# The maximum across blocks in a two-part attention and Fourier kernel: two transposes on TensorE in place of five small VectorE copies

## The chip, the cores and the metric

The kernel runs on one core of a Trainium2 chip. The metric is the device time of one execution in microseconds. Three runs of the kernel before took 1163.07 us in the median (1162.79 to 1165.32).

A core has five engines, each with its own queue of instructions that it works through in order: TensorE (PE) multiplies matrices and writes to PSUM, VectorE (DVE) and ScalarE (ACT) work on rows and read or write PSUM and SBUF, GpSimd (POOL) works on SBUF alone, and SyncE (SP) issues the transfers (DMA) here. They wait for each other by semaphores. PSUM has eight banks of 128 partitions x 512 floats. A matrix product holds one operand, the weights, in the array (its load is PEld in the profile) and streams the other.

## The reference, cut to what matters

```python
# part A: Fourier mixing, real part of a DFT over hidden (448) and sequence (2048)
a = einsum("bsd,ed->bse", x, dft_hid_re);  b = einsum("bsd,ed->bse", x, dft_hid_im)
y = einsum("ts,bse->bte", dft_seq_re, a) - einsum("ts,bse->bte", dft_seq_im, b)
# part B: attention, 16 heads of 28
q, k, v = split(x @ wqkv)
p = softmax(einsum("bhqd,bhkd->bhqk", q, k) * 28 ** -0.5)
o = einsum("bhqk,bhkd->bhqd", p, v)  ->  @ wo
out = concatenate([y, attention], axis=-1)       # (1, 2048, 896), float32
```

The inputs of part B are scaled by 8 each, so the scores are large and the softmax needs the maximum of each query's row.

## The kernel before, in words

Products are made in split precision: an operand is divided into a high part and a remainder, and two or three products are summed. Part A (`hidden`, `sequence`, lines 547 and 662) and the projections of part B (`project`, `values`, line 547) run as fill work in two PSUM banks (`fill_s`); the attention uses the other six (`bank_s`).

The attention is cut into units (h, c): a head and a chunk of 512 queries, 64 in all. Twenty units are `unit_twice`: the scores are computed once with queries on partitions for their maxima (line 754, maximum at 758), the maxima are transposed on TensorE (line 717), and the scores are computed again with the maximum subtracted inside the product (line 786). The other 44 are `unit_kept`, where the change lies. There the scores are computed once, keys on partitions and queries along the row: 16 tiles of 128 keys x 512 queries (line 808). ScalarE copies each tile to SBUF (line 813, through the helper at 415), and VectorE keeps a running elementwise maximum `rm` (lines 815 and 818), so `rm[p, n]` is the maximum over all keys whose number is p modulo 128.

What remains is a maximum over the 128 partitions for each query, and its spread to all partitions. Before, VectorE does all of it, in two PSUM banks `o` and `pm`. Number the queries n = 32 j + c (j below 16, c below 32) and the partitions p = 32 i + r (i below 4, r below 32).

1. Line 823 transposes `rm` in blocks of 32 x 32: `o[32 i + c, 32 j + r]` is the maximum of query 32 j + c at partition 32 i + r.
2. Line 825 takes the maximum over r and negates it: `pm[32 i + c, j]`, 128 x 16. What is left is a minimum over the four blocks i of partitions.
3. Line 830, three copies: blocks 1, 2 and 3 of 32 partitions are put beside block 0. Line 835 takes the minimum over the four: 32 x 16.
4. Line 833, two copies: the result is copied from 32 partitions to 64 and from 64 to 128.
5. Line 841 transposes in blocks once more, each column repeated 32 times, so that every partition of `pm` holds the negated maximum of all 512 queries.

ScalarE copies `pm` to `mb` in SBUF (line 843). GpSimd adds `mb` to the kept scores (line 858), or VectorE adds `pm` for some pairs of tiles; ScalarE takes the exponential (line 862); TensorE multiplies by the values (line 735, `pv_group`), in the narrow form of 32 columns of weights. `unit_out` copies the result out and `out_of` (877) folds and scales it.

The order of all instructions is written out before the launch by a list scheduler, `Schedule.run`. Each step has a cost on its engine, a latency after which others see it (`lat`), and a due time (`key`); of the steps that are ready on an engine, the one due first is taken. `RAW` is the time that the scheduler leaves after a VectorE step before a VectorE step that depends on it (`own=RAW`). `LANES`, `FLOW` and the `extra` of a transfer say when the scheduler thinks that a transfer lands. `Piece` (lines 515 to 537) loads a block of weights: a transfer to `wraw`, ScalarE's copy to `whi` (line 516), GpSimd's remainder `wlo` (line 522). In `project`, ScalarE copies a finished bank's high part (line 588) and VectorE writes the remainder (line 589), which frees the bank.

Of the kernel before, what the change touches and what calls it, by code (L numbers as in the profile page):

```python
# [11 lines left out]
F32 = mybir.dt.float32  # L12
F32R = mybir.dt.float32r
AF = mybir.ActivationFunctionType
ALU = mybir.AluOpType
AX = mybir.AxisListType
# [8 lines left out]
P = 128  # L25
NT = S // P
# [21 lines left out]
def f32(ap):  # L48
    return ap.bitcast(F32)
# [4 lines left out]

RAW = 0.16
LANES = 8
FLOW, FLOW_IN = 200.0, 400.0
T_IN = 20.0  # L60
# [257 lines left out]
def tile_kernel(ctx, tc, xa, wre, wim, wd, xb, wqkv, wo, out):  # L318
    nc = tc.nc
# [5 lines left out]
    sch = Schedule()  # L325

    def new(name, shape, dtype=F32, n=None, in_turn=False):
        if n is None:
            return sb.tile(shape, dtype, tag=name, name=name)
        sch.pools.append(Slots([sb.tile(shape, dtype, tag=f"{name}{i}", name=f"{name}{i}") for i in range(n)], in_turn))  # L330
        return sch.pools[-1]
# [10 lines left out]
    ident = new("ident", [P, P])  # L342
# [14 lines left out]
    sm_s = new("sm", [P, NT], F32, 1)  # L357
    mx_s = new("mx", [P, 4, NC], F32, 1)
    nm_s = new("nm", [P, 4], F32, 3)
    n2_s = new("n2", [64, P], F32R, 1)  # L360
    banks = [ps.tile([P, CH], F32, tag=f"bank{i}", name=f"bank{i}") for i in range(8)]

    w_first = Weights(lent, held=True)
# [23 lines left out]


    M512, M448, MS = 0.2335, 0.2065, 0.2365
    ACT_P, ACT_S, DVE_P, POOL_2, SMALL = 0.48, 0.52, 0.60, 1.25, 0.11  # L390

    def pe(key, emit, n=1, d=MS, lat=0.25, **kw):
        return sch.add({"PE": n * d}, key, emit, lat=lat, **kw)

    def dma(key, emit, size=256, extra=0.0, n=1, **kw):

        return sch.add({"SP": 0.4}, key, lambda e: emit(), dmas=[(size, extra)] * n, **kw)
# [4 lines left out]
    def dve(key, emit, d=DVE_P, **kw):  # L402
        return sch.add({"DVE": d}, key, lambda e: emit(), **kw)
# [105 lines left out]
    class Piece:  # L509


        def __init__(self, src, key, kind="c", early=False):
            self.hi, self.lo = whi.slot(), wlo.slot()
            raw = wraw.slot()
            ld = dma(key, lambda: nc.sync.dma_start(raw.t, src()), acq=[raw])
            a = act(key + (0 if early else 1), lambda: nc.scalar.activation(self.hi.t, raw.t, AF.Copy), ACT_S,  # L516
                    deps=[ld], acq=[self.hi], use=[raw])
            at = key + (0 if early else 1.5)
            both = ("DVE",) if early else ("POOL",)
            e = {g: {"DVE": 0.8, "POOL": 1.25}[g] for g in both}  # L520
            n = 4 if kind == "c" else 3
            b = sch.add(e, at, lambda g: eng[g].tensor_tensor(  # L522
                self.lo.t[:, :n], raw.t[:, :n], f32(self.hi.t)[:, :n], op=ALU.subtract),
                deps=[a], acq=[self.lo], use=[raw, self.hi])
            self.ready, self.hi_ready, self.lo_ready = [b], a, [b]
            if kind == "x":
                self.ready.append(sch.add({g: {"DVE": 0.3, "POOL": 0.53}[g] for g in both}, at, lambda g: eng[g].tensor_tensor(
                    self.hi.t[64:, 3], raw.t[64:, 3], f32(self.hi.t)[64:, 3], op=ALU.subtract),
                    deps=[a], use=[raw, self.hi]))
            elif kind == "w":  # L530
                self.ready.append(sch.add({g: {"DVE": 0.3, "POOL": 0.53}[g] for g in both}, at, lambda g: eng[g].tensor_tensor(
                    self.lo.t[:64, 3], raw.t[:64, 3], f32(self.hi.t)[:64, 3], op=ALU.subtract),
                    deps=[a, b], use=[raw, self.hi, self.lo]))
                self.ready.append(sch.add({"DVE": 0.15, "POOL": 0.25}, at, lambda g: eng[g].memset(
                    f32(self.lo.t)[64:, 3], 0.0), deps=[b], use=[self.lo]))
                self.lo_ready = self.ready
# [258 lines left out]
    def unit_kept(u):  # L795
        h, c = u
        t_a, t_b, dt = due[u]
        q = q_s.slot()
        lq = load_q(u, q)
        rm, mb = rm_s.slot(), mb_s.slot()  # L800
        kept, cs = [], []
        for kt in range(NT):
            o = bank_s.slot()
            if kt % 2 == 0:
                kept.append(kept_s.slot())
            s = Half(kept[-1], kt % 2)
            key = t_a + kt * dt
            m = pe(key, lambda e, o=o, kt=kt: nc.tensor.matmul(  # L808
                o.t, KT[h][kt // 4].t[:KR, kt % 4 * P:(kt % 4 + 1) * P], q.t[:KR, :], start=True, stop=True),
                deps=[*lq, *got_k[h, kt // 4], before.get("ka")], use=[o, s.pair, rm, q, KT[h][kt // 4]])  # L810
            in_line("ka", m)
            cs.append(sch.add({"ACT": ACT_P, "DVE": DVE_P} if kt == 1 else {"ACT": ACT_P}, key - 20,
                              lambda e, o=o, s=s: copy_of(e, s.t, o.t), deps=[m], use=[o, s.pair], lock=[o]))
            if kt == 1:
                prev = dve(key - 20, lambda o=o, s=kept[0]: nc.vector.tensor_tensor(rm.t, o.t, s.t[:, 0, :], op=ALU.max),
                           deps=[m, cs[0]], use=[rm, o, kept[0]], lock=[o], own=RAW)
            elif kt:
                prev = dve(key - 20, lambda o=o: nc.vector.tensor_tensor(rm.t, o.t, rm.t, op=ALU.max),  # L818
                           deps=[m, prev], use=[rm, o], lock=[o], own=RAW)
        key = t_a + 16 * dt - 20  # L820

        o = bank_s.slot()
        t = dve(key, lambda o=o: nc.vector.transpose(o.t, rm.t), 0.64, deps=[prev], acq=[o], use=[rm])  # L823
        pm = bank_s.slot()
        r = dve(key, lambda o=o: nc.vector.tensor_reduce(
            pm.t[:, :NT], o.t.rearrange("p (j r) -> p j r", r=32), axis=AX.X, op=ALU.max, negate=True), deps=[t], use=[o, pm], own=RAW)


        def beside(i):
            return lambda: nc.vector.tensor_copy(pm.t[:32, i * NT:(i + 1) * NT], pm.t[32 * i:32 * i + 32, :NT])  # L830

        def back(n, o=o):
            return lambda: nc.vector.tensor_copy(o.t[n:2 * n, :NT], o.t[:n, :NT])
        r = [dve(key, beside(i), SMALL, deps=[r], use=[pm], own=RAW) for i in (1, 2, 3)]
        r = dve(key, lambda o=o: nc.vector.tensor_reduce(
            o.t[:32, :NT], pm.t[:32, :4 * NT].rearrange("p (i j) -> p j i", i=4), axis=AX.X, op=ALU.min), 0.17,
            deps=r, use=[pm, o], own=RAW)
        for n in (32, 64):
            r = dve(key, back(n), SMALL, deps=[r], use=[o], own=RAW)

        t = dve(key, lambda o=o: nc.vector.transpose(pm.t, o.t[:, :NT].unsqueeze(2).to_broadcast([P, NT, 32])), 0.64,  # L841
                deps=[r], use=[pm, o], own=RAW)
        ld = act(key, lambda: nc.scalar.activation(mb.t, pm.t, AF.Copy), deps=[t], use=[pm, mb], lock=[pm])  # L843
        po = bank_s.slot()
        last_pv = None
        pairs = NT // 2

        def over_pair(t):
            return bass.AP(tensor=t.tensor, offset=t.offset, ap=[t.ap[0], [0, 2], [1, CH]])

        for g in range(NT // GV):
            es = []
            for i in range(GV // 2 * g, GV // 2 * (g + 1)):
                s = kept[i]
                key = t_b + 2 * i * dt

                def shift(e, s=s):
                    eng[e].tensor_tensor(s.t, s.t, over_pair(pm.t if e == "DVE" else mb.t), op=ALU.add)  # L858
                on_dve = i < DVE_SHIFT or due[u][0] > T_END - LATE
                sh = sch.add({"POOL": 2.36, "DVE": 1.13} if on_dve else {"POOL": 2.36}, key, shift,  # L860
                             deps=[ld, t, cs[2 * i], cs[2 * i + 1]], use=[s, mb, *([pm] if on_dve else [])])
                es.append(act(key, lambda s=s: nc.scalar.activation(s.t, s.t, AF.Exp, scale=SCALE), 0.96, deps=[sh], use=[s]))  # L862
            last_pv = pv_group(u, g, kept[GV // 2 * g:GV // 2 * (g + 1)], [*es, last_pv], po, key)
        unit_out(u, po, last_pv, key - 20)
# [33 lines left out]
    o = bank_s.slot()  # L898
# [18 lines left out]
    key = fkey(0, 0)  # L917
# [5 lines left out]
    key = fkey(0, 0)  # L923
# [19 lines left out]
    for n, c in enumerate(LAST):  # L943
        raws = []
        for k in range(4):
            pair = kept_s.slot()
            raw = Half(pair, 0)
            key = T_OUT + n
            deps = [o_done[h, c] for h in range(H) if (h + 1) * DH > k * P and h * DH < (k + 1) * P] + [before["ka"]]
            if k < 3:  # L950
                ld = dma(key, lambda raw=raw, k=k, c=c: nc.sync.dma_start(raw.t, on_d[k * P:(k + 1) * P, c * CH:(c + 1) * CH]),
                         deps=deps, use=[pair])
            else:
# [3 lines left out]
                ld = dma(key, twice, 128, n=2, deps=deps, use=[pair])  # L957
            raws.append((raw, ld))
        for i in range(2):
            x = [kt_s.slot() for _ in range(4)]  # L960
            ready = []
            for k in range(4):
                raw, ld = raws[k]
# [69 lines left out]
```

## Time and profile before

| | |
|---|---|
| median of 3 runs | 1163.07 us |
| the profiled execution | 1163.75 us |
| its span, first to last instruction | 1161.9 us |
| mean granted TensorE clock | 0.999 |
| TensorE busy | 1145.3 us (99%) |
| VectorE busy | 1010.8 us (87%) |
| ScalarE busy | 1029.1 us (89%) |
| GpSimd busy | 884.6 us (76%) |

In the profile an engine's busy time is the time in which it has an instruction in work. TensorE's products overlap, and their ends are modelled, so the distance between the starts of two products is a better measure of what one costs than its own length. A row of a group gives the line, the engine, the operation, the tiles out<-in, shapes and count, then the busy time, the mean length of one in ns, and the time that the engine had been idle before them, with what ended it. A row of the timeline gives the start, the length, and the instruction, and in brackets the idle time before it and what ended it. The second profile below has other line numbers: lines after 360 move by three, those after the reduction by one less.

### The profile page before, as it was taken

The numbers are of one execution on the slowest core, as the hardware profiler recorded it, in microseconds if no ns is written. First come the engines' busy times: TensorE is split into PE (matmuls) and PEld (weight loads), VectorE is DVE, ScalarE is ACT, GpSimd is POOL, SyncE is SP. The second block draws the span as 40 slices with busy tenths as digits, with TensorE's granted clock in tenths as the row PEclk, the third lists the DMA queues.
The fourth block names the chain that finished last, engine by engine and source line by source line (L and its number), as shares of the span: only waits on it lengthen the run. The fifth ranks groups of instructions, "written<-read, shape, count | busy, mean of one in ns | idle before, by whom it ended". The sixth has DMA issues, their size and how long they took to land.

```text
span 1161.9 us, 19485 instructions
## 1 busy us (share of the span) xinstructions
PE 1145.3 (99%) x6110; PEld 778.7 (67%) x6110; DVE 1010.8 (87%) x1803; ACT 1029.1 (89%) x1748; POOL 884.6 (76%) x521
## 2 busy tenths in 40 slices
PE   8999999999999999999999999999999999999998
PEld 7876556656676667767666656566666667766677
DVE  6599989999898989999899999998989998799832
ACT  5269999999999899999899999999999999899952
POOL 2138687888789888978888897987989899596630
PEclk9999999999999999999999999999999999999999
DMA  8893344222223222232333232232423223323543
GB/s 259 176 214 120 125 140 148 66 83 73 82 85 102 85 85 82 73 114 78 89 105 100 86 96 65 85 101 90 120 80 96 88 87 114 120 73 92 162 158 109
DMA packets 111880, 125.19 MB, mean 108 GB/s; under 512 B 49368, under 2 KB 63352, under 8 KB 111776
## 3 DMA queue, kind: packets, MB, share of 16 engines
q1 hardware_dynamic: 111776, 123.94, 35.8%
q8 instruction: 48, 0.79, 0.3%
q14 instruction: 56, 0.46, 0.1%
HBM read 90.00 MB, written 33.77 MB: 107 GB/s over the span
## 4 chain that ended last, share of the span: by engine, by line
PE 79%; DVE 9%; ACT 5%; DMA 3%; issue 3%; SPq 0%; DVEq 0%; ACTq 0%
PE bank L662 25%; PE bank L735 17%; PE bank L808 13%; PE bank L547 8%; PE bank L786 6%; PE bank L754 5%; DVE rm L818 4%; PE bank L987 3%; ACT kept L415 2%; DMA kept<-xb 1%; PE bank L877 1%; DVE mx L758 1%; ACT kept L790 1%; ACT kept L862 1%; DVE bank L823 1%
## 5 line engine op out<-in xcount | busy, mean ns | idle before, releaser
L858 POOL TENSOR_TENSOR kept<-kept,mb 128x1024 f32<-128x1024 f32 x254 | 605.7, 2409 | 93.7 <-ACT mb L843 85.6
L818 DVE TENSOR_TENSOR rm<-bank,rm 128x512 f32<-128x512 f32 x616 | 421.7, 685 | 53.7 <-PE bank L808 17.3
L415 ACT ACTIVATE kept<-bank 128x512 f32<-128x512 f32 (+1 forms) x661 | 381.0, 625 | 59.4 <-PE bank L808 34.4
L862 ACT ACTIVATE kept<-kept 128x1024 f32<-128x1024 f32 x341 | 361.2, 1102 | 7.8 <-DVE kept L858 5.0
L662 PE MATMUL bank<-big,whi 128*128 128x448 f32 x1024 | 325.3, 368 | 0.0
L522 POOL TENSOR_TENSOR wlo<-wraw,whi 128x512 fp32r<-128x512 f32 (+1 forms) x166 | 204.2, 1233 | 131.3 <-ACT whi L516 94.8
L808 PE MATMUL bank<-q,k 84*128 84x512 f32 x704 | 277.2, 414 | 2.6 <-DVE bank L841 1.6
L735 PE MATMUL bank<-kept,v 128*32 128x512 f32 x1944 | 240.7, 597 | 1.3 <-DVE mx L758 0.7
L758 DVE TENSOR_REDUCE mx<-bank 128x1 f32<-128x512 f32 x320 | 216.0, 681 | 8.6 <-PE bank L754 7.2
L662 PEld LDWEIGHTS bank<-big,whi 128*128 128x128 f32 x1024 | 193.3, 189 | 32.4 <-issue 5.9
L662 PE MATMUL bank<-big,wlo 128*128 128x448 f32 x512 | 188.4, 368 | 0.2 <-POOL wlo L522 0.2
L808 PEld LDWEIGHTS bank<-q,k 84*128 84x128 f32 x704 | 130.1, 189 | 86.8 <-issue 19.5
L790 ACT ACTIVATE kept<-bank 128x512 f32<-128x512 f32 x290 | 179.3, 637 | 4.1 <-PE bank L786 3.5
L735 PEld LDWEIGHTS bank<-kept,v 128*32 128x32 f32 x1944 | 56.4, 109 | 123.7 <-issue 110.9
L786 PE MATMUL bank<-q,k 86*128 86x512 f32 x320 | 127.4, 408 | 0.7 <-DMA q<-nmd 0.6
L754 PE MATMUL bank<-k,q 84*128 84x512 f32 x320 | 127.3, 407 | 0.3 <-DVE n L767 0.3
L516 ACT ACTIVATE whi<-wraw 128x512 fp32r<-128x512 f32 x167 | 110.8, 667 | 15.3 <-DMA wraw<-wqkv 12.1
L858 DVE TENSOR_TENSOR kept<-kept,bank 128x1024 f32<-128x1024 f32 x87 | 104.1, 1210 | 5.3 <-ACT mb L843 4.9
L662 PEld LDWEIGHTS bank<-big,wlo 128*128 128x128 f32 x512 | 96.9, 189 | 14.5 <-issue 1.0
L547 PE MATMUL bank<-wd,whi 128*128 128x448 f32 x256 | 79.6, 373 | 1.4 <-ACT kept L415 1.1
L786 PEld LDWEIGHTS bank<-q,k 86*128 86x128 f32 x320 | 59.8, 188 | 31.5 <-DVE rm L818 8.1
L754 PEld LDWEIGHTS bank<-k,q 84*128 84x128 f32 x320 | 60.0, 188 | 26.5 <-issue 4.2
(81 smaller groups left out, 1081.1 us busy)
## 6 DMA issues: line engine op xcount, KB each, us to landing
wraw<-wre SPq DMA_DIRECT2D x64, 256.0 KB
wraw<-wim SPq DMA_DIRECT2D x64, 256.0 KB
qkd<-wd SPq DMA_DIRECT2D x32, 256.0 KB
wraw<-xa SPq DMA_DIRECT2D x32, 256.0 KB
k<-qkd SPq DMA_DIRECT2D x64, 112.0 KB
q<-qkd SPq DMA_DIRECT2D x64, 112.0 KB
qkd<-kept SPq DMA_DIRECT2D x24, 256.0 KB
out<-kept SPq DMA_DIRECT2D x27, 224.0 KB
```

The lines of the kernel that those rows point to most:

```text
L415: nc.scalar.activation(dst, src, AF.Copy)
L522: b = sch.add(e, at, lambda g: eng[g].tensor_tensor(self.lo.t[:, :n], raw.t[:, :n], f32(self.hi.t)[:, :n], op=ALU.subtract), deps=[a], acq ...
L662: nc.tensor.matmul(o.t[:, :D], a.t[:, k, :], b[:, q * 4 + k, :], start=(q == 0 and k == 0 and j == 0), stop=(q == 3 and k == 3 and j == 2))
L735: nc.tensor.matmul(o.t[j * VW:(j + 1) * VW, :], VT[h].t[:, kt // 4, j, :], pairs[i // 2].t[:, i % 2, :], start=(kt < 4), stop=(kt >= NT - 4))
L754: m = pe(key, lambda e, o=o, kc=kc, qt=qt: nc.tensor.matmul(o.t, q.t[:KR, qt * P:(qt + 1) * P], KT[h][kc].t[:KR, :], start=True, stop=True ...
L758: ms.append(dve(key - 20, lambda o=o, kc=kc, qt=qt: nc.vector.tensor_reduce(mx.t[:, qt, kc:kc + 1], o.t, axis=AX.X, op=ALU.max), deps=[m], ...
L786: m = pe(key, lambda e, o=o, kt=kt: nc.tensor.matmul(o.t, KT[h][kt // 4].t[:KR + 2, kt % 4 * P:(kt % 4 + 1) * P], q.t[:KR + 2, :], start=T ...
L790: es.append(act(key - 20, lambda o=o, p=p: nc.scalar.activation(p.t, o.t, AF.Exp, scale=SCALE), deps=[m], use=[o, p.pair]))
L808: m = pe(key, lambda e, o=o, kt=kt: nc.tensor.matmul(o.t, KT[h][kt // 4].t[:KR, kt % 4 * P:(kt % 4 + 1) * P], q.t[:KR, :], start=True, sto ...
L818: prev = dve(key - 20, lambda o=o: nc.vector.tensor_tensor(rm.t, o.t, rm.t, op=ALU.max), deps=[m, prev], use=[rm, o], lock=[o], own=RAW)
L858: eng[e].tensor_tensor(s.t, s.t, over_pair(pm.t if e == "DVE" else mb.t), op=ALU.add)
L862: es.append(act(key, lambda s=s: nc.scalar.activation(s.t, s.t, AF.Exp, scale=SCALE), 0.96, deps=[sh], use=[s]))
```

## The change

Steps 3 and 4 above are replaced. The 128 x 16 maxima of step 2 are written to a small SBUF tile `m`. TensorE transposes it to 16 x 128 (`o[j, 32 i + c]`), so that the four blocks i lie beside each other along the row. One VectorE minimum over i reads them four times over (a broadcast axis) and writes 16 x 128 to the SBUF tile `mr`, already repeated for the four blocks of partitions. TensorE transposes this back to 128 x 16, into columns 128 to 143 of the bank `o`, and step 5 reads it from there. The tile `mr` shares a 128 x 128 tile, `small`, with `n2`, the maxima's tile of `unit_twice`: `n2` has partitions 0 to 63, `mr` has 64 to 79.

Two constants of the scheduler change too: `RAW` goes from 0.16 to 0.20, and the transfers of pieces due between 1 and 80 us are thought to land 6 us later.

```diff
-RAW = 0.16
+RAW = 0.20
...
-    n2_s = new("n2", [64, P], F32R, 1)
+    small = new("small", [P, P], F32R)
+    n2_s, mr_s = Slots([small[:64]]), Slots([f32(small)[64:64 + NT]])
+    sch.pools += [n2_s, mr_s]
+    m_s = new("m", [P, NT], F32, 1)
...
-            ld = dma(key, lambda: nc.sync.dma_start(raw.t, src()), acq=[raw])
+            ld = dma(key, lambda: nc.sync.dma_start(raw.t, src()), extra=6 if 1 < key < 80 else 0.0, acq=[raw])
...
         t = dve(key, lambda o=o: nc.vector.transpose(o.t, rm.t), 0.64, deps=[prev], acq=[o], use=[rm])
+        mq, mr = m_s.slot(), mr_s.slot()
+        r = dve(key, lambda o=o: nc.vector.tensor_reduce(
+            mq.t, o.t.rearrange("p (j r) -> p j r", r=32), axis=AX.X, op=ALU.max, negate=True), 0.61, deps=[t], use=[o, mq])
+
+        t = pe(key, lambda e, o=o: nc.tensor.transpose(o.t[:NT, :P], mq.t, ident), d=0.11, deps=[r], use=[o, mq])
+        r = dve(key, lambda o=o: nc.vector.tensor_reduce(
+            mr.t.rearrange("j (a c) -> j a c", a=4),
+            o.t[:NT, :P].rearrange("j (i c) -> j c i", i=4).unsqueeze(1).to_broadcast([NT, 4, 32, 4]), axis=AX.X, op=ALU.min),
+            0.62, deps=[t], use=[o, mr])
+        t = pe(key, lambda e, o=o: nc.tensor.transpose(
+            o.t[:, P:P + NT], mr.t, ident[64:64 + NT, 64:64 + NT]), d=0.11, deps=[r], use=[o, mr])
+
         pm = bank_s.slot()
-        r = dve(key, lambda o=o: nc.vector.tensor_reduce(
-            pm.t[:, :NT], o.t.rearrange("p (j r) -> p j r", r=32), axis=AX.X, op=ALU.max, negate=True), deps=[t], use=[o, pm], own=RAW)
-        def beside(i):
-            return lambda: nc.vector.tensor_copy(pm.t[:32, i * NT:(i + 1) * NT], pm.t[32 * i:32 * i + 32, :NT])
-        def back(n, o=o):
-            return lambda: nc.vector.tensor_copy(o.t[n:2 * n, :NT], o.t[:n, :NT])
-        r = [dve(key, beside(i), SMALL, deps=[r], use=[pm], own=RAW) for i in (1, 2, 3)]
-        r = dve(key, lambda o=o: nc.vector.tensor_reduce(
-            o.t[:32, :NT], pm.t[:32, :4 * NT].rearrange("p (i j) -> p j i", i=4), axis=AX.X, op=ALU.min), 0.17,
-            deps=r, use=[pm, o], own=RAW)
-        for n in (32, 64):
-            r = dve(key, back(n), SMALL, deps=[r], use=[o], own=RAW)
-        t = dve(key, lambda o=o: nc.vector.transpose(pm.t, o.t[:, :NT].unsqueeze(2).to_broadcast([P, NT, 32])), 0.64,
-                deps=[r], use=[pm, o], own=RAW)
+        t = dve(key, lambda o=o: nc.vector.transpose(pm.t, o.t[:, P:P + NT].unsqueeze(2).to_broadcast([P, NT, 32])), 0.64,
+                deps=[t], use=[pm, o])
```

2 lines of the change are left out of this document (1 added, 1 removed).

## The prediction

> **What bounds the kernel now.** I read the page from its top: shares of the span, the slices, the chain. Then the stretches of time, the waits of TensorE, and the groups that the change touches.
>
> ```profile
> PE 1145.3 (99%) x6110; PEld 778.7 (67%) x6110; DVE 1010.8 (87%) x1803; ACT 1029.1 (89%) x1748; POOL 884.6 (76%) x521
> ...
> PE   8999999999999999999999999999999999999998
> ...
> PE 79%; DVE 9%; ACT 5%; DMA 3%; issue 3%; SPq 0%; DVEq 0%; ACTq 0%
> ```
>
> TensorE is busy for 99% of the span, in every slice but the first and the last, and holds 79% of the chain. A busy TensorE need not be one at its peak, so the stretches and its waits come next (columns: window, length, busy time of PE, PEld, DVE, ACT, POOL with counts, clock, DMA share, GB/s).
>
> ```profile
> 100.00:200.00 100.00, 99.10 (x510) 60.47 (x508) 94.14 (x166) 94.60 (x162) 78.90 (x45) 1.00 0.39 135
> 200.00:300.00 100.00, 96.44 (x499) 62.64 (x496) 93.33 (x164) 95.68 (x167) 85.01 (x58) 0.98 0.24 71
> 300.00:500.00 200.00, 199.40 (x1108) 134.15 (x1110) 181.46 (x322) 190.67 (x320) 169.91 (x90) 1.00 0.29 88
> 900.00:1050.00 150.00, 150.00 (x834) 101.69 (x827) 134.67 (x243) 139.86 (x235) 128.83 (x69) 1.00 0.32 97
> ```
>
> From 300 us on TensorE hardly pauses (0.6 us in 200, none in 150), while VectorE has some 10% to spare. Who does hold TensorE up (waits of PE: for whom, us in total, times, longest)?
>
> ```profile
> PE bank L547 <- DVE kept L589: 2.5, 1, 2.5
> PE bank L808 <- DVE bank L841: 1.6, 2, 0.9
> PE bank L717 <- DVE nm L762: 1.5, 3, 0.6
> ...
> PE bank L735 <- DVE mx L758: 0.7, 1, 0.7
> ...
> PE bank L808 <- DVE mx L758: 0.6, 3, 0.2
> ```
>
> A single start-up wait of 2.5 us is the largest. So a time put on TensorE comes out at the end nearly whole, and a time taken off VectorE comes out only where one of these few waits hangs on it.
>
> **The change part by part.** *VectorE.* The groups that go, stay or serve as prices (busy us in total, mean ns of one, then idle before):
>
> ```profile
> L841 DVE STREAM_TRANSPOSE bank<-bank 128x512 f32<-128x512 f32 x44 | 32.2, 731 | 1.4
> L825 DVE TENSOR_REDUCE bank<-bank 128x16 f32<-128x512 f32 x44 | 30.7, 699 | 3.2 <-ACT kept L790 0.8
> L830 DVE COPY bank<-bank 32x16 f32<-32x16 f32 x132 | 23.5, 178 | 4.4
> L833 DVE COPY bank<-bank 32x16 f32<-32x16 f32 x88 | 15.7, 179 | 2.9
> L835 DVE TENSOR_REDUCE bank<-bank 32x16 f32<-32x64 f32 x44 | 9.5, 216 | 1.0
> ```
>
> The three copies of L830, the minimum of L835 and the two copies of L833 go, in each of 44 kept units: 3 x 0.178 + 0.216 + 2 x 0.179 = 1.11 us, 48.7 us in all. The new minimum reads 4 x 32 x 4 = 512 elements in 16 partitions and writes 128. Its price lies between L835 (64 elements read, 0.216) and L825 (512 read, 0.699); it reads as many as L825, so I take 0.70, or 30.8 us. VectorE gets 17.9 us lighter (at most 39). Both block transposes and the maximum that feeds them stay at their rows' prices; that the maximum now writes SBUF I count as nothing, bounded by 0.1 us each way (VectorE's spare tenth covers it; uncovered it would be 4 us).
>
> What of these 17.9 us reaches the end? Of TensorE's waits above, those on VectorE other than the start-up one sum to 1.6 + 1.5 + 0.7 + 0.6 = 4.4 us; the 1.5 are priced apart below, and of the other 2.9 I take half: -1.5 us, bounds 0 and -2.9. The tiles `m` and `mr` exist once each; with 44 reductions spread over some 1000 us no unit waits for them.
>
> *TensorE.* Two transposes per unit are new, 88 in all. The program of before has one of their kind, L717, which transposes 128x4 maxima against the identity. Its 20 records read 272 ns, but what matters is by how much it spreads the matmuls around it:
>
> ```profile
> 639.84 0.57 PE L662 MATMUL bank<-big,whi 128*128 128x448 f32 x2
> 640.25 0.37 PE L662 MATMUL bank<-big,wlo 128*128 128x448 f32 x1
> 640.46 0.27 PE L717 MATMUL bank<-ident,nm 128*4 128x128 f32 x1
> 640.48 0.66 PE L662 MATMUL bank<-big,whi 128*128 128x448 f32 x2
> 640.98 0.37 PE L662 MATMUL bank<-big,wlo 128*128 128x448 f32 x1
> ```
>
> Two matmuls start in the 0.41 us from 639.84 to 640.25: 0.205 each. From 640.25 to 640.98 three start, which without L717 would be 0.615; it is 0.73. So L717 costs TensorE 0.11 us, not 0.27. The first new transpose (128x16 against the identity) is that instruction with 12 more columns: 0.11. The second has 16 rows at partition 64 as its weights, 128 columns of them, and streams 16 columns. No row shows such a form. From below: L717's successor is issued 0.02 us after it, so 0.02. From above: as dear as L717 and a change into and out of the narrow form of L735 together:
>
> ```profile
> 636.09 0.36 PE L662 MATMUL bank<-big,whi 128*128 128x448 f32 x1
> 636.39 1.92 PE L735 MATMUL bank<-kept,v 128*32 128x512 f32 x16
> 638.24 0.47 PE L662 MATMUL bank<-big,whi 128*128 128x448 f32 x1
> ...
> 147.60 1.85 PE bank L735 x16
> ...
> 164.49 3.57 PE bank L735 x32
> ```
>
> Going in takes 0.30 instead of 0.205, so 0.09. Sixteen more records add 3.57 - 1.85 = 1.72 us, so a group on its own pays 1.85 - 1.72 = 0.13 on the way out (the last two rows are from the chain in order of time). That makes 0.11 + 0.09 + 0.13 = 0.33. I take 0.11, since L717 is nearest in operation and size. Together 88 x 0.11 = +9.7 us; bounds 44 x (0.11 + 0.02) = 5.7 and 88 x 0.33 = 29. Nothing hides it, as TensorE is the engine without gaps.
>
> The Trainium skill, page TensorEngine Tiling, section Tiling Modes, says that changing the tiling mode drains TensorE. By that rule each of the 88 would pay the way in and out, and the sum would be the upper bound. L717's form 128*4 beside 128*128 pays only 0.11 in all, so the trace does not bear the rule out for a small transpose; for the new form with few rows no run shows it yet.
>
> *The new waits.* Today the reduction runs on VectorE alone; now TensorE, which takes its instructions in order, must wait twice per unit for VectorE, with the fill work (L662, L547) and the scores (L808, L754, L786) queued behind. L717 is in that place now: 1.5 us of waits in 20, 0.075 each. 88 x 0.075 = +6.6 us. The second is tighter. In the order in which the changed program's instructions stand, six to eight matmuls lie between the two transposes in most units, about 1.3 to 1.7 us, in which the first must end (0.27), VectorE must take up the minimum (0.70) and release TensorE (0.14, from the end of L762 to L717 below). That is 1.11 us if VectorE is free at once. A VectorE instruction in front (0.69, L589 below) uses the slack up and costs a few tenths.
>
> ```profile
> 134.64 0.39 PE L547 MATMUL bank<-big,wlo 128*128 128x512 f32 x1
> 135.47 0.27 PE L717 MATMUL bank<-ident,nm 128*4 128x128 f32 x1 [0.44 <-DVE nm L762]
> ...
> 286.42 0.27 PE L717 MATMUL bank<-ident,nm 128*4 128x128 f32 x1 [0.50 <-DVE nm L762]
> ...
> 135.17 0.16 DVE L762 TENSOR_REDUCE nm<-mx 128x4 f32<-128x16 f32 x1
> 136.65 0.68 DVE L589 TENSOR_TENSOR wd<-bank,wd 128x512 fp32r<-128x512 f32 x1
> ```
>
> Bounds: 0, since two of L717's three waits (these rows) fall before 300 us, and 44 x 0.4 = 18 us. VectorE too now waits for TensorE at the minimum; behind it stand the maxima of L818 and L758, which free banks. Its spare tenth covers this.
>
> *The planner's constants.* `RAW` 0.20 spaces dependent VectorE steps wider in the plan; no instruction is added, and I price it at nothing (bounds 2 us either way, the size of one mishap such as the 2.5 us wait above). `extra=6` tells the planner that the early weight pieces land late. It moves one thing that I can see: in the changed order on ScalarE the second projected bank's copy (L588) stands ahead of the second piece's copy (L516), not behind it.
>
> ```profile
> 28.00 0.39 PE L547 MATMUL bank<-big,wlo 128*128 128x512 f32 x1
> 30.86 1.09 PE L547 MATMUL bank<-wd,big 128*128 128x448 f32 x4 [2.47 <-DVE kept L589]
> ...
> 26.62 0.63 ACT L516 ACTIVATE whi<-wraw 128x512 fp32r<-128x512 f32 x1 [7.04 <-DMA wraw<-wqkv]
> 28.96 0.63 ACT L516 ACTIVATE whi<-wraw 128x512 fp32r<-128x512 f32 x1 [1.72 <-DMA wraw<-wqkv]
> 29.50 1.06 ACT L588 ACTIVATE kept<-bank 128x512 fp32r<-128x512 f32 x2
> ```
>
> Before, L588 waits behind a piece that lands at 28.96, and TensorE waits for L589 behind it till 30.86. Moved ahead, L588 can start near 27.2 and L589 end near 28.5, so about 2.1 of the 2.5 us go; what is late next is the bank that the other L588 empties, needed only 2.25 us later (eleven matmuls). -2.1 us, bounds 0 and -2.5.
>
> *DMA.* No transfer is added. On SP's queue a few early loads of q and k pass stores of v and back; the DMA holds 3% of the chain, and the first scores start only at 39.55 us:
>
> ```profile
> 39.55 0.39 PE L808 MATMUL bank<-q,k 84*128 84x512 f32 x1
> ```
>
> Nothing, bounded by 1 us, since TensorE has project and value products to run in that time.
>
> **Sum.** +9.7 + 6.6 - 1.5 - 2.1 = +12.7 us. The profiled execution took 1163.75 us (span 1161.9), 0.7 above the median of 1163.07, so the change is put on the median: 1175.8 us. With the waits at their bounds of 0 and 18 us in place of 6.6, the likely case itself lies between 1169 and 1187 us.
>
> **The rivals.**
> 1. *The transposes pay for their change of form.* All 88 at 0.33: 29.0 + 6.6 - 3.6 = +32, so 1195 us. For it: L735's groups do pay. Against it: L717 does not. Chance 0.12. The rule of the Trainium skill named above (TensorEngine Tiling, Tiling Modes) is this case.
> 2. *The transposes slip in nearly free.* 5.7, no waits, and both reliefs whole: 5.7 - 2.9 - 2.5 = +0.3, so 1163.4. For it: the matmul after L717 is issued at once. Against it: the measured spread of 0.11. Chance 0.11.
> 3. *VectorE, not TensorE, paces the middle, and the change is faster.* VectorE is busy 94% between 100 and 300 us, and its rows hold 9% of the chain. Were all 17.9 us to reach TensorE, which needs every unit's relief to end a wait of TensorE: 9.7 + 6.6 - 2.1 - 17.9 = -3.7, so 1159.4. It decides from 14.2 us of the 17.9. Against it: TensorE's listed waits on VectorE are a fourth of that. Chance 0.16.
>
> My forecast has 0.61. Less than 0.2% (2.3 us) can't be told from no change here. Rival 3 is faster; rival 2 is split between same and slower, and a little of either side comes to same: faster 0.17, same 0.08, slower 0.75. The range that leaves out about a tenth at each end reaches from rival 3's time, 1160, to half way into rival 1, 1189.
>
> **What would show it.** Right: VectorE about 18 us less busy; L717's new siblings each spread their neighbours by 0.11; TensorE's busy time up by about 10 us and its waits on the two transposes at some 7; the pause at 28.4 us gone. Wrong: matmuls after the second transpose starting 0.3 us late (rival 1), TensorE's span shorter while the counts rise (rival 3), or the new waits far above 0.075 each, above all at the second transpose.

## The result, and the profile after

The changed kernel takes 1173.24 us in the median (1172.05 to 1174.76, six runs) against 1163.28 us for the kernel before: 10.0 us more, a ratio of 1.0081 with a 95% interval of 1.0068 to 1.0095. The forecast was slower, by 12.7 us. The profiled execution took 1172.05 us, its span 1170.3. The experiments below were timed on several chips, each with its own runs of the kernel before: beside experiments 9 and 10, twelve of nineteen such runs had a mean granted clock of 0.996 or 0.997 and took 1165.3 to 1167.6 us, and seven had 0.999 or 1.000 and took 1161.6 to 1164.9, so a ratio hangs by up to some 0.3% on which of these stood beside it.

The page of the changed kernel, with the engines' busy time and the chain that ended last:

```profile
PE 1154.7 (99%) x6198; PEld 791.4 (68%) x6198; DVE 987.9 (84%) x1576; ACT 1031.3 (88%) x1752; POOL 898.1 (77%) x524
...
PE 92%; ACT 3%; DVE 2%; DMA 1%; issue 1%; SPq 0%; POOL 0%; DVEq 0%; ACTq 0%; POOLq 0%
```

TensorE has 9.4 us more, VectorE 22.9 us less. VectorE's share of the chain fell from 9% to 2%: in the forecast's view the chain was TensorE's already, and now it is nearly all TensorE's. The waits of TensorE (for whom, us in total, times, longest) and some stretches:

```profile
PE bank L757 <- DMA q<-qkd: 5.9, 1, 5.9
...
PE bank L811 <- DVE kept L857: 0.5, 1, 0.5
PE bank L550 <- DVE kept L592: 0.5, 2, 0.2
...
PE bank L836 <- DVE small L832: 0.4, 1, 0.4
```

```profile
36.00:38.00 2.00, 2.00 (x10) 1.47 (x8) 0.47 (x3) 0.10 (x1) 0.00 (x0) 1.00 0.90 282
38.00:44.00 6.00, 0.13 (x2) 0.16 (x1) 0.00 (x0) 0.50 (x1) 0.00 (x0) 0.84 0.50 161
44.00:50.00 6.00, 6.00 (x18) 5.25 (x19) 2.65 (x8) 0.81 (x2) 0.00 (x0) 0.59 1.14 183
200.00:300.00 100.00, 99.39 (x533) 64.86 (x533) 94.09 (x150) 97.76 (x170) 87.33 (x60) 1.00 0.27 78
300.00:500.00 200.00, 200.00 (x1115) 135.06 (x1117) 177.72 (x278) 189.16 (x317) 175.47 (x92) 1.00 0.29 88
900.00:1050.00 150.00, 150.00 (x834) 101.69 (x827) 134.67 (x243) 139.86 (x235) 128.83 (x69) 1.00 0.32 97
```

The new waits at the two transposes are all but absent (0.4 us). In their place stands one pause that the forecast did not have: 5.9 us for the second q at 38 us, in which TensorE's clock falls. The granted clock is 0.50 from 42.08 to 48.92 us (0.59 in the row of the 6 us behind the pause), so some 2.5 us more are lost. The Trainium skill (page TensorE: Matmul & The Clock Gate, section The HAM clock gate) says that an idle window of about 3.4 us halves the clock until a busy window has passed; the 5.9 us pause and the low clock behind it agree. In every trace here a stretch of low clock lasts 3.4 or 6.8 us, unless the trace ends in it. The kernel before has one too, in the middle, which costs it some 1.7 us:

```profile
288.70:292.12 3.42, 3.42 (x10) 2.92 (x9) 3.26 (x5) 3.14 (x5) 3.42 (x2) 0.50 0.23 77
```

It stands behind waits of TensorE of only 0.50 and 0.92 us; in the ten microseconds ahead of it no two products start more than 1.4 us apart. So a single pause of 3.4 us is not needed for it here.

*What the transposes cost.* The timeline of TensorE around one second transpose:

```profile
339.41 0.57 PE L665 MATMUL bank<-big,whi 128*128 128x448 f32 x2
339.82 0.37 PE L665 MATMUL bank<-big,wlo 128*128 128x448 f32 x1
340.12 0.23 PE L836 MATMUL bank<-ident,small 16*128 16x16 f32 x1
340.27 0.67 PE L665 MATMUL bank<-big,whi 128*128 128x448 f32 x2
340.78 0.40 PE L811 MATMUL bank<-q,k 84*128 84x512 f32 x1
```

Three products of 448 columns start between 339.82 and 340.78; without L836 they would take 0.615 us, and they take 0.96. So it costs 0.35 us, though its record is only 230 ns long. L836 starts 0.30 us after the product ahead instead of 0.205, the same 0.09 more that the way into a narrow group costs; the next product starts 0.16 us behind it, and the one after that 0.10 us late. Over the 32 second transposes that stand between ordinary products the median is 0.355 (middle half 0.352 to 0.357); behind a narrow group, where a change of form is paid anyway, it is 0.26. The first transpose, worked out in the same way, costs 0.11, as L717 does.

*The account.* The same comparison can be made for all products: the distance between two starts against the usual one for that pair (0.205 us after 448 columns, 0.235 after 512, 0.093 more into a narrow group, 0.522 at the end of one). What a start is late beyond 0.03 us is counted as a pause, what lies around the transposes (old and new) on its own. Products at half the clock count as late, too. These sums are worked out from all starts of a trace, and another choice of the usual distances moves a term by about 1 us; in us, first to last start:

| | before | after | after, no 6 us (e2) | full form (e1) | order kept, no transposes (e8) | before, no small steps (e9) | RAW 0.16, no 6 us (e6) |
|---|---|---|---|---|---|---|---|
| products at their usual distance | 1113.8 | 1114.5 | 1114.5 | 1114.4 | 1115.0 | 1113.8 | 1113.7 |
| around transposes, waits included | 5.2 | 23.8 | 23.8 | 15.6 | 4.2 | 3.0 | 32.2 |
| pauses to 100 us | 8.1 | 13.1 | 7.2 | 13.7 | 14.9 | 5.8 | 9.4 |
| pauses, 100 to 1050 us | 29.2 | 11.8 | 11.2 | 13.7 | 20.1 | 20.6 | 14.3 |
| pauses after 1050 us, and the rest | 0.2 | 1.6 | 2.1 | 2.6 | 2.0 | 0.8 | 2.0 |
| first to last start | 1156.6 | 1164.8 | 1158.8 | 1160.1 | 1156.1 | 1144.2 | 1171.7 |

So the 8.2 us between the two traces are 18.6 more for transposes and 5.0 more at the start, less 17.4 of small pauses in the middle, with some 2 us elsewhere. The forecast had the sign and roughly the sum, but not these terms. The experiments take them one by one.

### The profile page after: what moved, and what is told of

Read it like the earlier page. It is cut to its first block, busy times and chain, and to the rows that moved or that the text cites. A ratio compares the mean times of both kernels' runs of the same rounds, so it can differ in the third digit from the quotient of the medians.

```text
span 1170.3 us, 19414 instructions
## 1 busy us (share of the span) xinstructions
PE 1154.7 (99%) x6198; PEld 791.4 (68%) x6198; DVE 987.9 (84%) x1576; ACT 1031.3 (88%) x1752; POOL 898.1 (77%) x524
## 4 chain that ended last, share of the span: by engine, by line
PE 92%; ACT 3%; DVE 2%; DMA 1%; issue 1%; SPq 0%; POOL 0%; DVEq 0%; ACTq 0%; POOLq 0%
PE bank L665 26%; PE bank L738 19%; PE bank L811 14%; PE bank L550 13%; PE bank L789 7%; PE bank L757 7%; PE bank L986 3%; PE bank L876 1%; DVE rm L821 1%; ACT kept L861 1%; ACT kept L418 1%; PE bank L836 1%; PE bank L831 1%; DMA kept<-xb 0%; ACT kept L793 0%
## 5 line engine op out<-in xcount | busy, mean ns | idle before, releaser
L857 POOL TENSOR_TENSOR kept<-kept,mb 128x1024 f32<-128x1024 f32 x259 | 618.1, 2409 | 93.0 <-ACT mb L842 87.6
L861 ACT ACTIVATE kept<-kept 128x1024 f32<-128x1024 f32 x342 | 362.6, 1098 | 10.1 <-POOL kept L857 7.2
L811 PE MATMUL bank<-q,k 84*128 84x512 f32 x704 | 269.2, 409 | 0.7 <-DVE kept L857 0.5
L761 DVE TENSOR_REDUCE mx<-bank 128x1 f32<-128x512 f32 x320 | 216.8, 683 | 21.6 <-PE bank L757 19.7
L811 PEld LDWEIGHTS bank<-q,k 84*128 84x128 f32 x704 | 130.0, 189 | 54.8 <-issue 10.1
L857 DVE TENSOR_TENSOR kept<-kept,bank 128x1024 f32<-128x1024 f32 x83 | 99.9, 1211 | 1.7 <-ACT mb L842 1.3
```

What stands on the lines that cost most here:

```text
L761: ms.append(dve(key - 20, lambda o=o, kc=kc, qt=qt: nc.vector.tensor_reduce(mx.t[:, qt, kc:kc + 1], o.t, axis=AX.X, op=ALU.max), deps=[m], ...
L811: m = pe(key, lambda e, o=o, kt=kt: nc.tensor.matmul(o.t, KT[h][kt // 4].t[:KR, kt % 4 * P:(kt % 4 + 1) * P], q.t[:KR, :], start=True, sto ...
```

## The experiments

My theory after reading the trace (A): the second transpose is dear because of its form; the pause for q comes from the constant `extra=6`; and a lighter VectorE takes away many small pauses that the list of waits doesn't show. The rivals: the transposes lie beside other work and the pause explains all (B); the planner's `RAW` did it (C); it is chance in the plan (D). Line numbers shift by a few from run to run.

**1. The second transpose in another form.** The data stay in 16 rows of the tile `small`, but all 128 rows are transposed.

```diff
+    nc.gpsimd.memset(f32(small), 0.0)
...
-            o.t[:, P:P + NT], mr.t, ident[64:64 + NT, 64:64 + NT]), d=0.11, deps=[r], use=[o, mr])
+            o.t[:, P:2 * P], f32(small), ident), d=0.11, deps=[r], use=[o, mr])
...
-        t = dve(key, lambda o=o: nc.vector.transpose(pm.t, o.t[:, P:P + NT].unsqueeze(2).to_broadcast([P, NT, 32])), 0.64,
+        t = dve(key, lambda o=o: nc.vector.transpose(pm.t, o.t[:, P + 64:P + 64 + NT].unsqueeze(2).to_broadcast([P, NT, 32])), 0.64,
```

> The changed kernel with the second transpose alone in another form: the whole 128 x 128 tile small (zeroed once at the start) is transposed against the whole identity, and the block transpose reads columns 192 to 207. The order of the instructions is the changed kernel's. Theory A (the second transpose costs TensorE 0.355 us because it sits in 16 rows at partition 64, and that is paid in full): in the full form the spread falls to 0.11 to 0.20 us, and the time to 1173.2 - 36 x 0.25 = 1164, between 1162 and 1167. Rival B (the slowdown is the 6 us pause for q at 38 us and the low clock after it, and the transposes lie beside other work): no change, 1171 to 1175.

Measured: 1167.88 us, ratio to the kernel before 1.0029 (1.0014 to 1.0045). The timeline of TensorE at the same unit:

```profile
339.98 0.36 PE L667 MATMUL bank<-big,wlo 128*128 128x448 f32 x1
340.18 0.27 PE L838 MATMUL bank<-ident,small 128*128 128x128 f32 x1
340.20 0.65 PE L667 MATMUL bank<-big,whi 128*128 128x448 f32 x2
340.69 0.39 PE L813 MATMUL bank<-q,k 84*128 84x512 f32 x1
```

From 339.98 to 340.69 it is 0.71 instead of 0.615: 0.10, and 0.110 in the median of 32. An instruction with eight times the rows, and eight times the columns streamed, costs a third. The order of TensorE's products is the same in both traces. The transposes' sum falls by 8.2 us; the time falls by 5.4 (4.7 between the two traces), as 3.5 come back as pauses. The time lies between the two ranges: B falls, and A's mechanism stands, but not its claim that all is paid at the end. The run changes rows, streamed columns and place in the array together, so which of them the price hangs on isn't shown.

**2. Without the 6 us.**

```diff
-            ld = dma(key, lambda: nc.sync.dma_start(raw.t, src()), extra=6 if 1 < key < 80 else 0.0, acq=[raw])
+            ld = dma(key, lambda: nc.sync.dma_start(raw.t, src()), acq=[raw])
```

> The changed kernel without the 6 us that the planner adds to the early pieces' landing. Theory A: the load of q goes ahead of the third load of k again, so the pause of 6.0 us at 38 us and the low clock behind it (about 3 us) go, and the 2.5 us pause at 28 us comes back: 1173.2 - 9 + 2.3 = 1166.5, between 1164 and 1169. Rival B (pauses at the start are made up later): 1171 to 1175. If the slowdown were nothing but this constant, the time would be at or below the kernel before's, 1163.

Measured: 1168.16 us, 1.0036 (1.0022 to 1.0049). The account shows the pauses of the first 100 us fall from 13.1 to 7.2 and nothing else move. A holds, with 5 us where 6.7 were expected. The pause at 28 us comes back, but only with 0.69 us in this trace, since the second piece lands earlier.

**3. The 6 us alone, on the kernel before.**

```diff
-            ld = dma(key, lambda: nc.sync.dma_start(raw.t, src()), acq=[raw])
+            ld = dma(key, lambda: nc.sync.dma_start(raw.t, src()), extra=6 if 1 < key < 80 else 0.0, acq=[raw])
```

> The kernel before with the changed kernel's 6 us on the early pieces and nothing else. Theory A (this constant alone puts the load of q behind the third load of k): the pause for q at 38 to 44 us and the low clock after it come, the pause at 28.4 us goes: 1163.5 + 9 - 2 = 1170, between 1167 and 1173. Rival (the load of q is late because of the new reduction): no pause, 1160 to 1163.

Measured: 1169.42 us, 1.0044 (1.0027 to 1.006). The same wait stands in its list, with the old reduction:

```profile
PE bank L754 <- DMA q<-qkd: 5.9, 1, 5.9
```

Theory A holds: the pause has nothing to do with the transposes.

**4. RAW alone, on the kernel before.**

```diff
-RAW = 0.16
+RAW = 0.20
```

> The kernel before with RAW = 0.20 and nothing else. Theory A (the relief comes from VectorE's lighter load): within 2 us of the kernel before, 1161 to 1165. Rival C (the wider spacing in the plan is what lets TensorE load its weights in time): 1150 to 1159.

Measured: 1169.17 us, 1.0052 (1.0031 to 1.0073). Neither fits. The small pauses stay as they were (28.9 us between 100 and 1050), so RAW alone doesn't take them away. Between the traces it is 4.4 us from first to last start: the plan enters a narrow group 117 times instead of 109, at some 0.2 us each (0.093 on the way in, 0.522 instead of 0.41 at the end), and behind 1050 us it has a wait that the kernel before hasn't:

```profile
PE bank L877 <- DVE ou L417: 2.0, 1, 2.0
```

**5. Both constants as before, so the new reduction alone.**

```diff
-RAW = 0.20
+RAW = 0.16
...
-            ld = dma(key, lambda: nc.sync.dma_start(raw.t, src()), extra=6 if 1 < key < 80 else 0.0, acq=[raw])
+            ld = dma(key, lambda: nc.sync.dma_start(raw.t, src()), acq=[raw])
```

> The changed kernel with RAW = 0.16 and without the 6 us, so the new reduction alone. Theory A (costs add up: the 6 us were worth 5 us, RAW 0.20 was worth 5.5 us on the kernel before): 1173.2 - 5 - 5.5 = 1162.7, so about as fast as the kernel before, 1160 to 1165, though TensorE has 20 us more to do. Rival D (RAW 0.20 hurts only the kernel before, where ten VectorE steps are spaced by it, or by chance of the plan): 1166 to 1171.

Measured: 1176.61 us, 1.0098 (1.0076 to 1.012). Neither theory has it: the costs do not add up, and it is slower than D's range too. From experiment 2 to this one only RAW changes, and the time rises by 8.4 us (by 7.2 going by the two ratios, as the runs are from two chips). The two traces are 12.9 us apart, and 8.4 of that lies around the transposes (23.8 to 32.2), 3.1 in the middle and 2.2 at the start. The waits show where about half of the 8.4 comes from:

```profile
PE bank L831 <- DVE m L828: 2.8, 4, 1.9
...
PE bank L720 <- DVE nm L765: 1.4, 1, 1.4
```

With 0.16 the plan puts the first transpose where VectorE is not ready. So 0.20 hurt the kernel before and helped the new reduction. Only these two values were run, each with one plan, so whether the spacing as such does it or the chance of a plan (D) isn't shown.

**6. The same, with the full form.** All of experiment 1's edit and both constants:

```diff
-RAW = 0.20
+RAW = 0.16
...
-            ld = dma(key, lambda: nc.sync.dma_start(raw.t, src()), extra=6 if 1 < key < 80 else 0.0, acq=[raw])
+            ld = dma(key, lambda: nc.sync.dma_start(raw.t, src()), acq=[raw])
...
-            o.t[:, P:P + NT], mr.t, ident[64:64 + NT, 64:64 + NT]), d=0.11, deps=[r], use=[o, mr])
+            o.t[:, P:2 * P], f32(small), ident), d=0.11, deps=[r], use=[o, mr])
```

> As the run before, with the second transpose in the full 128 x 128 form. Theory A (5 to 6 us less, as with the new constants): 1157, between 1154 and 1160, faster than both kernels. Rival (under the old constants TensorE is not what paces): no different from the run with the narrow form.

Measured: 1172.38 us, 1.0055 (1.0036 to 1.0075): 4.2 us below the narrow form, so the form is paid here too, but far from 1157; the same waits at the first transpose stand in its list (2.8 us).

**7. Planned without transposes.** The two `pe(...)` steps are taken out before the planner runs, so that it plans anew (VectorE's steps, which now depend on each other, get the spacing `own=RAW`).

```diff
-        t = pe(key, lambda e, o=o: nc.tensor.transpose(o.t[:NT, :P], mq.t, ident), d=0.11, deps=[r], use=[o, mq])
+        t = r
...
-        t = pe(key, lambda e, o=o: nc.tensor.transpose(
-            o.t[:, P:P + NT], mr.t, ident[64:64 + NT, 64:64 + NT]), d=0.11, deps=[r], use=[o, mr])
+        t = r
```

> The changed kernel without its two TensorE transposes: VectorE does the same work (block transpose, maximum, minimum over 512 in 16 partitions, block transpose), the minimum reads the bank as it is and the last block transpose reads the tile m, so the maximum is not taken across the four blocks of partitions. Theory A: 1173.2 - 19.7 (transposes) - 2 (their waits) = 1151, between 1147 and 1156, which is 12 us below the kernel before although the pause for q stays: that is the relief of a lighter VectorE and of the planner's constants. Rival B (transposes lie beside other work): 1168 to 1174.

Measured: 1168.18 us, 1.0032 (1.0015 to 1.0048), where rival B expected it. But the plan had changed: pauses between 100 and 1050 us were 27.7 us against 11.8, and the clock is 0.50 for 3.42 us at three places there (from 295.7, 712.1 and 766.8 us). It shows what a new plan can do, and does not price the transposes. So:

**8. The order kept.** The steps stay in the plan and in the order; only their instructions are left out.

```diff
-        t = pe(key, lambda e, o=o: nc.tensor.transpose(o.t[:NT, :P], mq.t, ident), d=0.11, deps=[r], use=[o, mq])
+        t = pe(key, lambda e: None, d=0.11, deps=[r], use=[o, mq])
...
-        t = pe(key, lambda e, o=o: nc.tensor.transpose(
-            o.t[:, P:P + NT], mr.t, ident[64:64 + NT, 64:64 + NT]), d=0.11, deps=[r], use=[o, mr])
+        t = pe(key, lambda e: None, d=0.11, deps=[r], use=[o, mr])
```

> The changed kernel in its own order, with both transposes left out of TensorE's queue at their places (the last block transpose reads the tile m, so the maximum is not taken across the four blocks). Here the plan can't change. Theory A (the transposes are paid in full): 1173.2 - 19.7 - 2 = 1151.5, between 1149 and 1155. Rival B (half of what TensorE gives back is lost to waits for the other engines, as in the planned run without transposes): 1158 to 1167.

Measured: 1163.52 us, 0.9992 (0.9979 to 1.0005). Rival B's half: TensorE has 19.6 us less around transposes, and the time falls by 9.7. The order of the other products is the same. The account shows where the rest went: pauses in the middle rise from 11.8 to 20.1 us. Some 2.3 us of that are only moved: they stand behind narrow groups, where the changed kernel has a transpose. Of the rest, the pauses at weight loads that VectorE held up rise from 2.9 to 6.3 us, at those that ScalarE held up from 1.1 to 3.1 (experiment 9 says how they are told). So while TensorE transposes, the other engines catch up.

**9. VectorE's relief alone.** The kernel before, its order kept, with the five copies and the small minimum left out.

```diff
-            return lambda: nc.vector.tensor_copy(pm.t[:32, i * NT:(i + 1) * NT], pm.t[32 * i:32 * i + 32, :NT])
+            return lambda: None
...
-            return lambda: nc.vector.tensor_copy(o.t[n:2 * n, :NT], o.t[:n, :NT])
+            return lambda: None
...
-        r = dve(key, lambda o=o: nc.vector.tensor_reduce(
-            o.t[:32, :NT], pm.t[:32, :4 * NT].rearrange("p (i j) -> p j i", i=4), axis=AX.X, op=ALU.min), 0.17,
+        r = dve(key, lambda: None, 0.17,
```

> The kernel before in its own order, with the five copies and the small minimum (L830, L833, L835) left out of VectorE's queue at their places; the last block transpose reads the 128 x 16 maxima, so the maximum is not taken across the four blocks of partitions. VectorE gets 48.7 us lighter, TensorE's work and the plan stay. Theory A (the short pauses of TensorE in the middle hang on VectorE's load): they fall by at least 9 us, to 1154, between 1150 and 1157. Rival E (only TensorE's listed waits on VectorE hang on it, 2.9 us): 1160 to 1163.

Measured: 1153.49 us, 0.9905 (0.9883 to 0.9928). Theory A. The steps left out took 48.7 us, and VectorE's busy time falls by 45.7; on an engine that was 87% busy and 9% of the chain they are worth about 11 us (0.95% of 1163), or 9.4 against the seven runs of the kernel before with a clock of 0.999 or more. The order of TensorE's products is the same. Of the 12.4 us between the traces 8.6 are pauses in the middle, just under the 9 that A asked for; the rest lies at the start and around the transposes. The waits of TensorE's weight loads show it, which the list of PE's waits left out. The kernel before, the changed kernel, and this one (the scores' loads that VectorE released, us, times, longest):

```profile
PEld bank L808 <- DVE rm L818: 13.3, 32, 0.8
...
PEld bank L808 <- DVE mx L758: 7.7, 22, 0.8
PEld bank L808 <- DVE bank L841: 7.0, 17, 1.2
```

```profile
PEld bank L811 <- DVE rm L821: 9.3, 17, 0.8
...
PEld bank L811 <- DVE mx L761: 1.9, 5, 0.8
```

```profile
PEld bank L809 <- DVE rm L819: 7.7, 15, 0.8
...
PEld bank L809 <- DVE bank L841: 4.2, 5, 0.8
PEld bank L809 <- DVE mx L759: 3.3, 10, 0.8
```

Over all the scores' loads (three lines in each kernel, waits above 0.15 us) it is 145 times, 66 and 83. The times in these rows are not TensorE's loss. What is lost is seen at the product behind: in the kernel before, between 100 and 1050 us, 89 ordinary products whose own load did not wait follow one whose load had waited for VectorE. Of these 63 start more than 0.05 us late, and the median is 0.097; of 2661 where neither load waited, 3 do. The products still overlap, so PE counts as busy throughout.

With this the pauses in the middle can be told apart. Those with a load that VectorE held up, at the late product or at the one ahead, sum to 13.8 us in the kernel before (110 starts), 2.9 in the changed kernel (25) and 6.5 in this one (47). In the plan of experiment 7, with the same light load on VectorE, they are 12.4: the order counts as much as the load. Another 10.1, 7.6 and 9.7 us (before, changed, this one) are no waits for others: the second product behind a narrow group starts 0.10 us late, on top of the 0.522 at its end.

**10. Can both costs be had back?** The changed kernel with the full form and without the 6 us, and the one with the full form, the 6 us, and the loads of the first q due earlier. The edits of experiments 1 and 2, and for the second kernel that of experiment 1 with this one:

```diff
-        return [dma(due[u][0] - 12, lambda: rows_of(q.t, 0, h * 2 * DH, c * CH, (c + 1) * CH),
+        return [dma(due[u][0] - (12 if due[u][0] > 40 else 18), lambda: rows_of(q.t, 0, h * 2 * DH, c * CH, (c + 1) * CH),
```

> The changed kernel with the second transpose in the full form and without the 6 us on the pieces. Theory A (the two costs are separate and add up): 1173.2 - 5.4 - 5.1 = 1162.7, between 1160 and 1165, which is the kernel before's time though VectorE has 18 us less to do. Rival D (chance of the plan): above 1166.

> The changed kernel with the second transpose in the full form, and with the loads of q for the first units due 18 us ahead instead of 12, so that the second q stands before the loads of k that it stood behind. Theory A (the pause for q is 4.4 us of waiting and some 2.5 us of low clock, and can be had back without giving up the 6 us on the pieces): 1167.9 - 7 = 1161, between 1158 and 1163, so a little faster than both kernels. Rival: the k loads, now later, hold TensorE up in the same place, 1165 to 1168.

Measured: 1161.19 us, 0.9971 (0.9957 to 0.9984), and 1159.22 us, 0.9954 (0.9939 to 0.997). Theory A both times. Both are a little faster than the kernel before, and the second is the fastest that was found. By the same account it has some 10 us more around the transposes than the kernel before, 16 less of pauses in the middle and 1 less at the start. In its stretches from 38 to 50 us TensorE doesn't pause, and the clock stays up:

```profile
38.00:44.00 6.00, 6.00 (x30) 5.35 (x29) 3.56 (x10) 1.79 (x3) 0.00 (x0) 1.00 0.68 220
44.00:50.00 6.00, 6.00 (x31) 5.34 (x29) 4.23 (x11) 1.95 (x4) 0.00 (x0) 1.00 1.11 189
```

**11. The same start with the old reduction.** The kernel before, with the 6 us and the q loads due earlier.

```diff
-            ld = dma(key, lambda: nc.sync.dma_start(raw.t, src()), acq=[raw])
+            ld = dma(key, lambda: nc.sync.dma_start(raw.t, src()), extra=6 if 1 < key < 80 else 0.0, acq=[raw])
...
-        return [dma(due[u][0] - 12, lambda: rows_of(q.t, 0, h * 2 * DH, c * CH, (c + 1) * CH),
+        return [dma(due[u][0] - (12 if due[u][0] > 40 else 18), lambda: rows_of(q.t, 0, h * 2 * DH, c * CH, (c + 1) * CH),
```

> The kernel before with the 6 us on the early pieces and with the loads of q for the first units due 18 us ahead, so with the same start as the fastest kernel so far, but the old reduction on VectorE. Theory A (the two start pauses go, the middle stays as it was): 1169.4 - 8 = 1161.5, between 1160 and 1163; then the new reduction in its full form, 1159.2, is itself worth about 2 us. Rival (all that the fastest kernel gained is its start): 1157 to 1159.5.

Measured: 1162.48 us, 0.9989 (0.9978 to 1.0001). Theory A again. So of the 0.46% that the fastest kernel gains, the start gives about 0.1, not clear of nothing, and the new reduction with its RAW and its plan the rest: 3.3 us between the two medians, which are from two chips.

## Why the prediction came out right

The direction and the size (12.7 forecast, 10.0 measured) were right, but large terms were missed on each side and cancelled. That the sum came so near was luck.

- *VectorE's work.* Forecast 17.9 us less, with the new minimum at 0.70. The minimum took 0.682 (30.0 us in all), so the reduction gave 18.7. VectorE's total fell by 22.9: the plan gave it 6 shifts of L858 fewer besides (83 and none on borrowed tiles, after 87 and 2), at 1.21 us each, and some 3 us more in other groups.

```profile
L832 DVE TENSOR_REDUCE small<-bank 16x128 f32<-16x512 f32 x44 | 30.0, 682 | 18.0 <-PE bank L831 17.1
L831 PE MATMUL bank<-ident,m 128*16 128x128 f32 x44 | 12.1, 275 | 0.0
L836 PE MATMUL bank<-ident,small 16*128 16x16 f32 x44 | 10.1, 230 | 0.5 <-DVE small L832 0.4
```

- *The first transpose*, 0.11 us by the distance of the starts around L717: right.
- *The second transpose* is the step that failed: "I take 0.11, since L717 is nearest in operation and size". It was near in operation and size, but not in form; it measured 0.355, just over the upper bound of 0.33, which was worked out from L735's changes of form. The rule of the Trainium skill that I weighed (TensorEngine Tiling, Tiling Modes: a change of tiling mode drains TensorE) agrees with this one: 16 rows at partition 64 between products of 128 rows pay 0.355, the full form 0.11. It does not show for the first, where only the columns are few: 0.11. So rival 1 was right for one transpose of the two. What sets that one apart from L735's groups, where also only the columns are few and 0.09 is paid on the way in, no run shows, and the profile doesn't tell the tiling mode. The 88 came to about 20 us, not 9.7.
- *"Nothing hides it"*: half wrong. In its own order 19.6 us of transposes are worth 9.7 us of time (experiment 8), since TensorE, though 99% busy, still held small pauses (29.2 us in the kernel before, 20.1 in experiment 8), of which those for the other engines shrink when they get more time.
- *The new waits*, 6.6 us. What is around the transposes in the changed kernel (23.8 us) less the transposes themselves (about 19.7 for the new, 2.2 for L720's 20) leaves 1.9. With RAW 0.16 it is 8.4 more. The forecast priced RAW at nothing, within 2 us, and the waits at 6.6; but RAW 0.20 cost the kernel before some 6 us (experiment 4) and saved the new reduction 7 to 8 (experiment 5).
- *What VectorE gives back*, -1.5 with bounds of 0 and -2.9: too small by far. The small pauses in the middle fell by 17.4. Of these, 10.9 stood at loads that VectorE held up (13.8 to 2.9); 1.5 were the low clock at 289 us, some 2.5 are the products behind narrow groups where a transpose stands now, and the rest is spread. With the transposes left out in the same order the 2.9 are 6.3, so 3.4 of the 10.9 come from the transposes' own time and 7.5 from the lighter VectorE and the new plan. Experiment 9 shows that VectorE's load alone does such a thing (7.3 us of these pauses for 45.7 us of work), and experiment 7 that a plan alone can undo it. How the 7.5 divide between the two isn't shown. Rival 3's mechanism was thus at work, if not enough to decide. The forecast looked at the list of PE's waits, which holds only pauses longer than the products' overlap; the waits of the weight loads had the others.
- *The pause at 28.4 us*, -2.1: right. The step at 30.86 us now starts at 28.71, with 0.20 us of wait. How much the constant saves varies with the landing of the pieces: without it the longest such wait is 0.69 us in experiment 2's trace and 2.6 in that of experiment 10's first kernel.

```profile
28.11 0.39 PE L550 MATMUL bank<-big,wlo 128*128 128x512 f32 x1
28.71 3.54 PE L550 MATMUL bank<-wd,big 128*128 128x448 f32 x16 [0.20 <-DVE kept L592]
```

- *DMA*, "nothing, bounded by 1 us, since TensorE has project and value products to run": wrong. TensorE works in order, and the first product that needs the second q stands ahead of those. The load was issued 7.5 us later than before, behind a load of k that itself waited for a store to land (SP's queue in the changed kernel, then before):

```profile
38.13 0.85 SPq L692 DMA_DIRECT2D k<-qkd  x1
...
40.54 0.47 SPq L692 DMA_DIRECT2D q<-qkd  x1
```

```profile
33.04 0.36 SPq L689 DMA_DIRECT2D q<-qkd  x1
```

  It cost 5.9 us and the low clock behind it. Experiments 2 and 3 put it at 5 to 5.5 us of the result, less than the 5.9 and some 2.5 us together: by the account, other pauses of the first 100 us are fewer with it.

## What to carry to other kernels

Price a small TensorE instruction by how far it pushes the starts of its neighbours apart, not by its record, and give it the array's full form when it stands between full products: here zeros in the rest of a tile cost less than a change of form. On an engine that is 99% busy, look at the waits of its weight loads as well as its own, and expect only part of what is added or removed to reach the end. When an issue moves on an in-order queue, find the first consumer in the consumer's order; whether other work exists doesn't matter if it stands behind.

## What the runs showed of the hardware that I had not expected

A TensorE transpose of 16 rows with 16 columns streamed costs 0.355 us between full products, and one of 128 by 128 costs 0.110. Where a wait holds a weight load back, the product behind starts about 0.1 us late (median 0.097 of 89), though its own record shows no idle time before it. A group in the narrow form makes the second product behind it 0.10 us late, too. And the granted clock falls to 0.50 for 3.4 or 6.8 us at a time: for 6.8 us after a wait of 5.9 us, and in the kernel before for 3.4 us behind waits of no more than 0.92 us.
